# Turned inverse transform, half of x turned on TensorE, and denominators spread through DRAM, in a kernel of a long convolution beside linear attention

## The chip, the cores and the metric

The kernel runs on one core of one Trainium2 chip. The metric is the device time of one execution in microseconds (us); the median of several is quoted. A profiled execution gives the span, which is about 2 us shorter than the time. In some executions of this kernel the granted clock of TensorE is lower and the time longer by some per cent; those are called slow and are not compared with fast ones. A run counts as slow when it is over 1.5% above the fastest of the same kernel. SBUF and PSUM are the two on-chip memories in which the program places its buffers; its matmuls write to PSUM.

## The reference, cut to what matters

Two independent halves are computed and put side by side in the output. All inputs and outputs are bf16; S = 2048 and D = 576.

```python
# half A: a short filter on k, a product with v, a long convolution, a product with q
kv = k_shift * v                                   # k_shift: four taps along S
y  = irfft(rfft(kv, 2 * S) * rfft(ssm_k, 2 * S))[:S] + kv * ssm_D
a  = q * y
# half B: linear attention, 32 heads of 18
phi = lambda t: where(t > 0, t + 1, exp(t)) + 1e-6
num = phi(q) @ (phi(k)^T v)          # for each head
den = phi(q) @ sum_s phi(k) + 1e-6   # one denominator for each row and head
b   = (num / den) @ wo               # q, k, v = x @ wqkv
out = concatenate([a, b], axis=-1)
```

## The kernel before

The kernel issues its operations from a fixed list, `PLAN`. Each word names an engine and an operation (`P` TensorE, `A` ScalarE, `D` VectorE, `G` GpSimd, `S` the engine that issues transfers, SyncE); a second list, `PLACES`, gives each buffer its place. Each engine works through its own words in order, so an operation that waits holds up all later ones on its engine. This order was tuned.

Half A runs as two stages of matmuls with tables (forward, for the filter "h" and for the input "u"), a product, and two inverse stages. Between the two inverse stages the data are turned by a DMA transpose:

```python
def inv(g, su, bias):                       # first inverse stage, for one of nine pieces
    ...                                     # products of the two transforms: tx and xb
    V = SB("V", [128, 2, 8, 128])
    for jp in range(2):
        for wi, (w, src) in enumerate(((W31, tx), (W32, xb))):
            for h in range(2):
                for g2 in range(2):         # the small table is stationary: 64x64 tiles
                    nc.tensor.matmul(ps..., lhsT=w()[64 * h:64 * h + 64, :], rhs=v[:, g2, ...])
        ...                                 # evicted to V
    turn("Vtr", Vt[hf]..., V)               # DMA transpose

def inv2(hf, bias):                         # last inverse stage
    vt = Vt[hf].t[:].rearrange("p g (h r t) -> p r (g h) t", h=2, t=2)
    ...
    nc.tensor.matmul(o, lhsT=Esb.t[:, b, ri, :], rhs=vt[:, 2 * b + ri, :], ...)
```

In half B the projections need x turned, which comes by DMA transposes, and the reciprocals of the denominators (32 rows for each group of 512 columns) must be repeated 18 times over the partitions. Matmuls with a 0/1 table do that, into PSUM, from where the multiplication reads them:

```python
def b_bc(c, gp):
    ps = psb(2, "bps")
    for j in range(2):                      # "spreading" matmuls
        nc.tensor.matmul(ps.t[0:hn, j, :], lhsT=esel()[...], rhs=rden.t[...])
    # VectorE: pqT = (pqT + EPS) * spread reciprocal
    nc.vector.scalar_tensor_tensor(out=o, in0=o, scalar=EPS, in1=ps.t[0:hn], op0=ALU.add, op1=ALU.mult)
```

Each output projection ("out", ten matmuls) needs five of the ten multiplications, and each multiplication serves eight projections. GpSimd takes some of the products of half A; one takes it about 4 us, against 1.2 us on VectorE.

Of the kernel before, what the change touches and what calls it, by code (L numbers as in the profile page):

```python
# [9 lines left out]
BF = mybir.dt.bfloat16  # L10
# [108 lines left out]
def _tables():  # L119
# [35 lines left out]
    C = np.zeros((128, 224 + 128 + 630 + 32 + 160 + 126 + 8), np.float32)  # L155
    C[:, 0:32] = np.tile(W[:, 0], (4, 1))
    for r in range(2):
        for t in range(2):
            C[64 * r + t:64 * r + 64:2, 32 + 32 * t:64 + 32 * t] = W[:, 0]
            for i in range(2):  # L160
                C[64 * r + 32 * t:64 * r + 32 * t + 32, 96 + 64 * i + t:160 + 64 * i:2] = W[:, 1 + i]
    o = 224
# [35 lines left out]
def _act(n):  # L198
    return 0.17 + n * 0.000868


def _dve(n, rate=1):
    return 0.145 + n * 0.001045 / rate
# [6 lines left out]
def _dma(nb, row=4096):  # L210
    return nb / (16.0 * row / (8.0 + row * 0.0412) * 1000.0)
# [3 lines left out]
def kernel(  # L215
# [18 lines left out]
    G_d = nc.inline_tensor(Gt.reshape(128, -1), name="tab_g").ap()  # L234
# [32 lines left out]
    cst = SB("cst", [128, Ct.shape[1]], side=1, pre=True)  # L267
    neg1 = SB("neg1", [128, 1], FP32, side=1, pre=True)
    Gsb = SB("Gsb", [128, 16, 2, 128], side=1, pre=True)
# [11 lines left out]
    def cs(o, n):  # L281
        return cst.t[:, o:o + n]
# [3 lines left out]
    W31 = lambda: cs(96, 64)  # L286
    W32 = lambda: cs(160, 64)
    ident = lambda: cs(224, 128)
    esel = lambda: cs(352, 630).rearrange("p (c m) -> p c m", c=5)
    sel127 = lambda: cs(982, 32)  # L290
    hmask = lambda: cs(1014, 160).rearrange("p (c m) -> p c m", c=5)
    maskbd = lambda: cs(1174, 126)
    epsc = lambda: cs(1300, 1)
# [7 lines left out]
    xTg = []  # L301
    xTt = SB("xTt", [128, S])

    def xt_tail():
        load("xTt", xTt, lambda e: nc.sync.dma_start_transpose(out=xTt.t[:], in_=x[:, 448:576]), 524288,
             wr=[(xTt, "t")], issue=2.2, row=512, gap=0.5)
        P.op(("POOL", 0.9), lambda e: nc.gpsimd.memset(xTt.t[0:1, :], 1.0), rd=[(xTt, "t")], wr=[(xTt, "t")],
             name="xT1", bias=900)

    def xt_load(g):  # L310
        b = SB("xT%d" % g, [128, 4, 512])
        xTg.append(b)
        load("xT", b, lambda e: nc.sync.dma_start_transpose(
            out=b.t[:], in_=x[512 * g:512 * g + 512, 0:512]), 524288, wr=[(b, "m")], issue=2.2, row=512, gap=0.5)
# [41 lines left out]
    cload = load("cst", cst, lambda e: dma(cst.t[:], C_d), 128 * 2 * Ct.shape[1], bias=("cst", 0.0))  # L356
# [3 lines left out]
    for hh in range(2):  # L360
# [6 lines left out]
        P.op(("PE", 1.2), wmm, rd=[srow, ones], wr=[wps], name="wj", bias=("wall", 0.0), cnt=4)  # L367
# [3 lines left out]
    kv_load(0)  # L371
    xt_tail()
# [7 lines left out]
    load("Gsb", Gsb, lambda e: dma(Gsb.t[:].rearrange("p a b c -> p (a b c)"), G_d), 1048576)  # L380
# [37 lines left out]
    def h_piece(i):  # L418
# [3 lines left out]
        for half in range(2):  # L422
# [12 lines left out]
            P.op(("PE", 8 * 0.081), tr, rd=[hs, cst], wr=[ps], use=[hT[cc]], name="htr", cnt=8, bias=("t%d" % cc, 0.0))  # L435
# [9 lines left out]
    TX, seq = {}, {}  # L445

    def s1(cc, nm, bias):
        C = SB("C" + nm, [128, CC // 2, 32, 2])
        for ri in range(2):
            for bg in range(2):  # L450
                ps = psb(3, "s1ps")

                def mm(e, ri=ri, bg=bg, ps=ps):
                    for j in range(8):
                        b = 8 * bg + j
                        src = hT[cc].t[:, b, :] if nm == "h" else vs[bg].t[:, j, CC * cc:CC * cc + CC]
                        for bank, lo, hi in banks(CC * j, CC * j + CC):
                            nc.tensor.matmul(ps.t[:, bank, lo - 512 * bank:hi - 512 * bank], lhsT=Gsb.t[:, b, ri, :],  # L458
                                             rhs=src[:, lo - CC * j:hi - CC * j], start=True, stop=True)
# [7 lines left out]
                P.op(("PE", 0.72), mm, rd=rdk + [Gsb], wr=[ps], use=[C], name="s1" + nm, cnt=10, bias=bias)  # L467
# [3 lines left out]
    def turn(name, dst, src, rd, wr, bias):  # L471

        load(name, None, lambda e: nc.sync.dma_start_transpose(out=dst(), in_=src()), 524288, rd=rd, wr=wr, bias=bias,
             issue=2.2, row=512, gap=0.5)

    def s2(C, cc, pp, nm, bias):
        nw = PCH // 2
        if nm == "u":
# [7 lines left out]
        else:  # L486
            ct = SB("ctH", [128, 16, 128])
            turn("turn", lambda: ct.t[:],
                 lambda: C.t[:, nw * pp:nw * pp + nw].rearrange("p w r t -> p (w r t)"), [C], [ct], bias)
        g = cc * (CC // PCH) + pp  # L490
        sp = SB("sp" + nm, [128, 16, 128])
        for kp in range(2):
            ps = psb(2, "s2ps")

            def mm(e, kp=kp, ps=ps):
                if nm == "u":
                    for j in range(4):
                        for kk in range(2):
                            kh = 2 * kp + kk
                            w0 = 16 * (j // 2)  # L500
                            nc.tensor.matmul(ps.t[32 * j:32 * j + 32, kk, :].rearrange("p (w k) -> p w k", w=16),  # L501
                                             lhsT=W2()[32 * kh:32 * kh + 32, :],
                                             rhs=ct.t[32 * kh:32 * kh + 32, w0:w0 + 16, :, j % 2], start=True, stop=True)
                else:
                    for r in range(2):
                        for h in range(2):
                            b0 = 8 * h + 4 * kp
                            nc.tensor.matmul(ps.t[64 * h:64 * h + 64, r, :].rearrange("p (b k) -> p b k", b=4),  # L508
                                             lhsT=W2D()[64 * r:64 * r + 64, :],
                                             rhs=ct.t[64 * r:64 * r + 64, b0:b0 + 4, :], start=True, stop=True)  # L510

            def ev(e, kp=kp, ps=ps):
                if nm == "u":
                    copy(e, sp.t[:, :, 64 * kp:64 * kp + 64].rearrange("p w (h k) -> p h w k", h=2),
                         ps.t.rearrange("p h (w k) -> p h w k", w=16))
                else:
                    copy(e, sp.t[:, 8 * kp:8 * kp + 8, :].rearrange("p (b r) k -> p r b k", r=2),
                         ps.t.rearrange("p r (b k) -> p r b k", b=4))
            aft = [seq[x] for x in (nm, ("h", g)) if x in seq] if kp == 0 else []
            last = P.op(("PE", T8), mm, rd=[ct, cst], wr=[ps], use=[sp], name="s2" + nm, bias=bias, cnt=8 if nm == "u" else 4,  # L520
# [8 lines left out]
    Vt = [SB("Vt%d" % i, [128, VN[i] // 4, 128], side=1) for i in range(2)]  # L529

    def inv(g, su, bias):
# [4 lines left out]
        load("X", xb, lambda e: dma(xb.t[0:128:2], tx.t[1:128:2]), 262144, rd=[tx], wr=[(xb, 0)], bias=bias, row=4096)  # L536
        load("X", xb, lambda e: dma(xb.t[1:128:2], tx.t[0:128:2]), 262144, rd=[tx], wr=[(xb, 1)], bias=bias, row=4096)
# [6 lines left out]
        V = SB("V", [128, 2, 8, 128])  # L544
        for jp in range(2):
            ps = psb(2, "i1ps")

            def mm(e, jp=jp, ps=ps):
                for wi, (w, src) in enumerate(((W31, tx), (W32, xb))):
                    for h in range(2):  # L550
                        for g2 in range(2):
                            v = src.t[64 * h:64 * h + 64].rearrange("p (w g) k -> p g w k", g=2)
                            nc.tensor.matmul(  # L553
                                ps.t[64 * g2:64 * g2 + 64, h, :].rearrange("p (w k) -> p w k", w=4),
                                lhsT=w()[64 * h:64 * h + 64, :], rhs=v[:, g2, 4 * jp:4 * jp + 4, :],
                                start=(wi == 0), stop=(wi == 1))
            P.op(("PE", 2 * T8), mm, rd=[tx, xb, cst], wr=[ps], use=[V], name="i1", bias=bias, cnt=8)
            P.op(either(1024), lambda e, jp=jp, ps=ps: copy(
                e, V.t[:, :, 4 * jp:4 * jp + 4, :].rearrange("p h w k -> p h (w k)"), ps.t), rd=[ps], wr=[(V, jp)],
                name="i1ev", bias=bias)  # L560
        turn("Vtr", lambda: Vt[hf].t[:, c0 // 4:c0 // 4 + 16, :], lambda: V.t[:].rearrange("p h w k -> p (h w k)"),
             [V], [(Vt[hf], g)], bias)

    def inv2(hf, bias):
# [6 lines left out]
        for bg in range(16 // nb):  # L571
            ps = psb(2, "i2ps")

            def mm(e, bg=bg, ps=ps):
                vt = Vt[hf].t[:].rearrange("p g (h r t) -> p r (g h) t", h=2, t=2)
                for j in range(nb):
                    o = ps.t[:, j // (nb // 2), n * (j % (nb // 2)):n * (j % (nb // 2)) + n].rearrange(
                        "p (g t) -> p g t", t=2)
                    for ri in range(2):
                        b = nb * bg + j  # L580
                        nc.tensor.matmul(o, lhsT=Esb.t[:, b, ri, :], rhs=vt[:, 2 * b + ri, :],  # L581
# [6 lines left out]
            P.op(("PE", 1.6 * _pe(*[n] * (2 * nb))), mm, rd=[Vt[hf], Esb], wr=[ps], name="i2", cnt=2 * nb, bias=bias)  # L588
# [11 lines left out]
    def kproj(r):  # L600
# [10 lines left out]
        P.op(("PE", _pe(*[HALF] * 10)), mm, rd=[xTg[r // 4], xTt, wk], wr=[ps], use=[eb], name="k", bias=("k", 0.0), cnt=10)  # L611
# [8 lines left out]
    def qproj(c, gp):  # L620
# [9 lines left out]
        P.op(("PE", _pe(*[512] * 10)), mm, rd=[xTg[2 * gp], xTg[2 * gp + 1], xTt, wq],  # L630
# [14 lines left out]
    for c in range(5):  # L645
# [4 lines left out]
    load("x", x_sb, lambda e: dma(x_sb.t[:, :, 0:D], ap(x, 0, [[D, 128], [128 * D, 16], [1, D]])), 2359296, row=1152,  # L650
         wr=[(x_sb, "x")], after=[k_ids[AFTER["x"]]])
    P.op(("POOL", 0.3), lambda e: nc.gpsimd.memset(x_sb.t[:, :, D:D + 1], 1.0), wr=[(x_sb, "o")], name="x1",
         bias=400, after=[k_ids[AFTER["x"]]])
# [5 lines left out]
    def b_G(t):  # L659
# [7 lines left out]
        P.op(("PE", _pe(*[HALF] * 32)), mm, rd=[x_sb, pk], wr=[ps], use=[GT, gcol], name="G", cnt=32, bias=("G", 0.0))  # L667
# [36 lines left out]
    P.op(("PE", 25 * 0.081), kvmm, rd=[wv5, GT], wr=[kps], use=[kvb], name="kv", cnt=25, bias=("G", 0.0))  # L704

    def kvev(e):
# [3 lines left out]
    P.op(("DVE", _dve(504)), kvev, rd=[kps, cst], wr=[(kvb, 0)], name="kvev", bias=("G", 0.0))  # L710
    P.op(("DVE", _dve(72)), lambda e: nc.vector.tensor_tensor(
        out=kvb.t[0:72, 4, 0:72], in0=kps.t[0:72, 1, 0:72], in1=maskbd()[0:72, 0:72], op=ALU.mult),
        rd=[kps, cst], wr=[(kvb, 1)], name="kvev", bias=("G", 0.0))
# [6 lines left out]
    P.op(("PE", 0.4), zmm, rd=[(GT, 4), cst], wr=[zps], use=[zsel], name="z", cnt=5, bias=("z", 0.0))  # L720
# [7 lines left out]
    P.op(("DVE", 0.3), zev, rd=[zps, cst], wr=[zsel], name="zev", bias=("z", 0.0))  # L728
# [14 lines left out]
    P.op(("PE", 1.2), dmm, rd=[zsel, pqT, cst], wr=[dps], use=[den, dcol, rden], name="den", cnt=40, bias=("z", 0.0))  # L743
# [11 lines left out]
    def b_M(c):  # L755
# [7 lines left out]
        P.op(("PE", _pe(HALF, HALF)), mm, rd=[kvb, wo5], wr=[ps], use=[M], name="M", cnt=2, bias=("G", 0.0))  # L763
# [4 lines left out]

    def b_bc(c, gp):
        h0, hn = HCH[c]  # L770
        ps = psb(2, "bps")

        def mm(e):
# [136 lines left out]
```

## Time and profile before

| | before |
|---|---|
| time, median of 3 runs | 183.16 us (182.57 to 186.32; the last counts as slow) |
| span of the profiled run | 180.0 us |
| TensorE, VectorE, ScalarE, GpSimd busy | 161.2, 143.7, 109.8, 46.5 us |
| first matmul of k's projection | 17.23 us |
| first matmul of G = x^T phi(k) | 69.12 us |
| first output projection | 120.52 us |
| last matmul ends | 176.36 us |

In the views, PE is TensorE, PEld its weight loads, DVE VectorE, ACT ScalarE, POOL GpSimd and SP SyncE, and L607 is line 607 of that version's program. The busy time of an engine is read against the span; the windows show in which stage an engine is full; the chain of work that ended last shows what the end was waiting for. The four moments in the last rows cut the kernel into stages that can be compared between versions. "End minus first G" is used below as the length of the second part: here 180.03 - 69.12 = 110.91 us.

### The profile page before, as it was taken

The page shows a single profiled execution, that of the slowest core. Times are in us where ns is not written, and L with a number is a line of the kernel's source. Part 1 is how long each engine was busy: PE and PEld are TensorE (multiplying, and loading weights), DVE is VectorE, ACT ScalarE, POOL GpSimd, SP SyncE. Part 2 cuts the span into 40 slices and gives each one's busy share as a digit, 9 for nine tenths or more (in the row PEclk, how much of TensorE's full clock was granted, in tenths as well). Part 3 has the DMA queues.
Part 4 walks back from the last instruction along what each step waited for, and adds up shares of the span by engine and source line. Part 5 has one row for each costly group of instructions (what it writes and reads, how often), then busy time and mean ns, then how long its engine had stood idle before and what let it go on. Part 6 is the DMA issues. An engine that isn't in the chain of part 4 may idle for free.

```text
span 180.0 us, 3538 instructions
## 1 busy us (share of the span) xinstructions
PE 161.2 (90%) x1448; PEld 104.5 (58%) x1448; DVE 143.7 (80%) x136; ACT 109.8 (61%) x118; POOL 46.5 (26%) x29
## 2 busy tenths in 40 slices
PE   0795999999999979899999978788799999999991
PEld 0664677754766757676677745433348565554450
DVE  0307589898979899899969899996968999686863
ACT  2083364648856788755668889995958798620000
POOL 8004000150080340006304960653882000000000
PEclk9999799999999999999999999978969999999999
DMA  5999799999999944998096019979399983999844
GB/s 181 327 202 283 143 298 422 298 169 263 336 237 350 378 164 93 179 283 253 29 304 226 15 22 206 239 124 233 97 346 259 222 183 120 259 208 273 261 142 149
DMA packets 68886, 39.49 MB, mean 219 GB/s; under 512 B 50375, under 2 KB 66373, under 8 KB 68230
## 3 DMA queue, kind: packets, MB, share of 16 engines
q1 hardware_dynamic: 68870, 39.27, 84.9%
q8 instruction: 11, 0.18, 0.4%
q14 instruction: 5, 0.04, 0.1%
HBM read 17.77 MB, written 4.72 MB: 125 GB/s over the span
## 4 chain that ended last, share of the span: by engine, by line
PE 74%; DVE 9%; ACT 6%; DMA 6%; issue 2%; SPq 0%; DVEq 0%
PE ps_all L628 12%; PE ps_all L607 12%; PE ps_all L795 11%; PE ps_all L665 11%; PE ps_all L581 9%; PE ps_all L458 5%; PE ps_all L553 4%; PE ps_all L429 3%; DVE pqT L782 3%; DMA hs<-in_A_ssm_k_dram 3%; DMA wk<-in_B_wqkv_dram 3%; ACT Ch L253 2%; PE ps_all L508 2%; DVE Cu L255 2%; PE ps_all L501 2%
## 5 line engine op out<-in xcount | busy, mean ns | idle before, releaser
L407 POOL TENSOR_TENSOR v<-m,v 128x1536 bf16<-128x1536 bf16 x5 | 17.0, 3408 | 55.9 <-DVE m L404 26.2
L795 PE MATMUL ps_all<-M,pqT 126*128 126x288 bf16 (+1 forms) x160 | 24.3, 306 | 0.0
L253 ACT ACTIVATE sph<-ps_all 128x1024 bf16<-128x1024 f32 x18 | 18.0, 1022 | 8.4 <-PE ps_all L508 7.4
L607 PE MATMUL ps_all<-wk,xT 128*128 128x288 bf16 x128 | 21.4, 301 | 1.1 <-DMA wk<-in_B_wqkv_dram 1.1
L458 PEld LDWEIGHTS <-Gsb 128*128 128x128 bf16 x240 | 17.4, 102 | 7.4 <-issue 6.0
L396 DVE TENSOR_TENSOR m<-kh,Wj 128x3072 bf16<-128x3072 bf16 x12 | 20.8, 1748 | 0.9 <-DMA kh<-in_A_k_dram 0.9
L628 PE MATMUL ps_all<-xT,wq 128*126 128x512 bf16 (+1 forms) x80 | 20.7, 381 | 0.0
L665 PE MATMUL ps_all<-pk,x_sb 128*128 128x288 bf16 (+1 forms) x160 | 20.6, 287 | 0.0
L795 PEld LDWEIGHTS <-pqT 126*128 126x128 bf16 (+1 forms) x160 | 15.7, 103 | 8.3 <-issue 3.7
L253 ACT ACTIVATE spu<-ps_all 128x1024 bf16<-128x1024 f32 x16 | 15.8, 1026 | 4.9 <-PE ps_all L501 4.3
L665 PEld LDWEIGHTS <-x_sb 128*128 128x128 bf16 x160 | 15.3, 98 | 5.1 <-issue 1.3
L612 ACT ACTIVATE ek<-ps_all,neg 128x576 bf16<-128x576 f32 x16 | 11.8, 744 | 10.2 <-PE ps_all L607 5.3
L628 PEld LDWEIGHTS <-wq 128*126 128x126 bf16 (+1 forms) x100 | 12.7, 131 | 7.9 <-issue 0.9
L607 PEld LDWEIGHTS <-xT 128*128 128x128 bf16 x128 | 13.1, 103 | 5.5 <-issue 1.2
L581 PE MATMUL ps_all<-Vt,Esb 128*128 128x320 bf16 (+1 forms) x64 | 15.9, 421 | 0.0
L253 ACT ACTIVATE V<-ps_all 128x1024 bf16<-128x1024 f32 x13 | 12.9, 1022 | 4.1 <-PE ps_all L553 4.0
L632 ACT ACTIVATE eq<-ps_all,neg 126x1024 bf16<-126x1024 f32 (+1 forms) x10 | 11.1, 1112 | 6.4 <-PE ps_all L628 6.4
L586 DVE TENSOR_TENSOR q<-ps_all,q 128x640 bf16<-128x640 f32 (+1 forms) x12 | 11.2, 954 | 4.4 <-PE ps_all L581 4.4
L253 ACT ACTIVATE Ch<-ps_all 128x1536 bf16<-128x1536 f32 x9 | 13.0, 1501 | 1.8 <-PE ps_all L458 1.8
L615 DVE SCALAR_TENSOR_TENSOR pk<-ek,ps_all 128x576 bf16<-128x576 bf16 x16 | 11.8, 751 | 2.4 <-ACT ek L612 2.4
L635 DVE SCALAR_TENSOR_TENSOR pqT<-eq,ps_all 126x1024 bf16<-126x1024 bf16 (+1 forms) x10 | 12.2, 1215 | 1.7 <-ACT eq L632 1.5
L782 DVE SCALAR_TENSOR_TENSOR pqT<-pqT,ps_all 126x1024 bf16<-126x1024 bf16 (+1 forms) x10 | 11.9, 1212 | 1.6 <-PE ps_all L776 1.4
(77 smaller groups left out, 257.9 us busy)
## 6 DMA issues: line engine op xcount, KB each, us to landing
X<-sph SPq DMA_DIRECT2D x18, 256.0 KB, 3.9
hs<-in_A_ssm_k_dram SPq DMA_DIRECT2D x6, 384.0 KB, 4.1
v<-in_A_v_dram SPq DMA_DIRECT2D x2, 1152.0 KB, 9.6
x_sb<-in_B_x_dram SPq DMA_DIRECT2D x1, 2304.0 KB
out_dram<-ob SPq DMA_DIRECT2D x16, 144.0 KB, 3.1
kh<-in_A_k_dram SPq DMA_DIRECT2D x1, 1584.0 KB
q<-in_A_q_dram SPq DMA_DIRECT2D x1, 1280.0 KB
out_dram<-q SPq DMA_DIRECT2D x4, 320.0 KB, 2.6
```

What stands on the lines that cost most here:

```text
L253: nc.scalar.activation(out=o, in_=i, func=ACTF.Copy)
L396: nc.vector.tensor_tensor(out=m.t[:, i:i + 2], in0=i0, in1=i1, op=ALU.mult)
L407: lambda e: vec(e).tensor_tensor(out=vt.t[:, :, c0:c0 + CC], in0=m.t[:, 0], in1=vt.t[:, :, c0:c0 + CC], op=ALU.mult),
L458: nc.tensor.matmul(ps.t[:, bank, lo - 512 * bank:hi - 512 * bank], lhsT=Gsb.t[:, b, ri, :], rhs=src[:, lo - CC * j:hi - CC * j], start=Tru ...
L581: nc.tensor.matmul(o, lhsT=Esb.t[:, b, ri, :], rhs=vt[:, 2 * b + ri, :], start=(ri == 0), stop=(ri == 1))
L607: nc.tensor.matmul(ps.t[:, hh, 0:HALF], lhsT=xs(t, 128 * r, 128), rhs=wk.t[:, t, HALF * hh:HALF * hh + HALF], start=(t == 0), stop=(t == 4))
L612: P.op(("ACT", _act(576) + 0.085), lambda e: nc.scalar.activation(out=eb.t[:], in_=ps.t[:, :, 0:HALF], func=ACTF.Exp, bias=neg1.t[:]), rd= ...
L628: nc.tensor.matmul(ps.t[0:hn, j, :], lhsT=wq.t[:, t, h0:h0 + hn], rhs=xs(t, 1024 * gp + 512 * j, 512), start=(t == 0), stop=(t == 4))
L635: P.op(("DVE", _dve(1024)), lambda e: nc.vector.scalar_tensor_tensor(out=pqT.t[0:hn, c, 1024 * gp:1024 * gp + 1024].rearrange("p (h c) -> ...
L665: nc.tensor.matmul(ps.t[:, hh, 0:n], lhsT=x_sb.t[:, r, FT[t]:FT[t] + 128], rhs=pk.t[:, r, HALF * hh:HALF * hh + n], start=(r == 0), stop=( ...
L782: nc.vector.scalar_tensor_tensor(out=o, in0=o, scalar=EPS, in1=ps.t[0:hn], op0=ALU.add, op1=ALU.mult)
L795: nc.tensor.matmul(ps.t[:, hh, 0:HALF], lhsT=pqT.t[0:hn, c, 128 * r:128 * r + 128], rhs=M.t[0:hn, c, HALF * hh:HALF * hh + HALF], start=(c ...
```

## The change

The intent is to take work and hops off TensorE and the DMA queue. There are five parts.

1. In the first inverse stage the products become stationary and the table moves. The result comes out turned already, so the DMA transposes of V go, and the last inverse stage reads another layout.
2. The reciprocals are stored to DRAM and loaded back with a repeating address, in place of the spreading matmuls. The multiplication then reads them from SBUF.
3. "u" is turned on VectorE for six of nine pieces; the other three (`UT`) go by DMA transpose.
4. x is loaded early in its plain layout, its column of ones is written ahead of it, and the first half of it (`XP = 2` of four groups) is turned on TensorE.
5. The order and the places are made anew.

```diff
 def inv(g, su, bias):
-        V = SB("V", [128, 2, 8, 128])
         for jp in range(2):
-                for wi, (w, src) in enumerate(((W31, tx), (W32, xb))):
-                    for h in range(2):
-                        for g2 in range(2):
-                            nc.tensor.matmul(..., lhsT=w()[64 * h:64 * h + 64, :], rhs=v[:, g2, 4 * jp:4 * jp + 4, :], ...)
+                for j in range(8):
+                    for wi, src in enumerate((tx, xb)):
+                        nc.tensor.matmul(ps.t[:, j // 4, 128 * (j % 4):128 * (j % 4) + 128],
+                                         lhsT=src.t[:, 8 * jp + j, :], rhs=W3(wi), start=(wi == 0), stop=(wi == 1))
-        turn("Vtr", lambda: Vt[hf].t[:, c0 // 4:c0 // 4 + 16, :], ...)
 def inv2(hf, bias):
-                vt = Vt[hf].t[:].rearrange("p g (h r t) -> p r (g h) t", h=2, t=2)
+                vt = Vt[hf].t[:].rearrange("p r (g b t) -> p r b g t", g=2, t=2)
 ...
 def b_bc(c, gp):
-        ps = psb(2, "bps")
-            ... nc.tensor.matmul(ps.t[0:hn, j, :], lhsT=esel()[32 * g:32 * g + 32, c, 0:hn], rhs=rden.t[...])
+            bt = SB("bct", [128, 2, 512])
+            load("bc", bt, lambda e: dma(bt.t[0:hn]..., ap(
+                rdd, 14 * c * S + 1024 * gp, [[S, hn // 9], [0, 9], [1, 1024]])), ...)
-            nc.vector.scalar_tensor_tensor(out=o, in0=o, scalar=EPS, in1=ps.t[0:hn], op0=ALU.add, op1=ALU.mult)
+            nc.vector.scalar_tensor_tensor(out=o, in0=o, scalar=EPS, in1=bt.t[0:hn], op0=ALU.add, op1=ALU.mult)
 ...
 def xt_load(g):
+        if g >= XP: ... DMA transpose as before; return
+                        nc.tensor.transpose(out=..., in_=x_sb.t[:, 4 * g + 2 * hf + r, c0:c0 + 128], identity=ident())
 ...
+UT = (1, 4, 7)
+XP = 2
+BCD = 1
 PLAN = ...     # all words new
 PLACES = ...   # all places new
```

## The prediction

> **What bounds the kernel now.** I read the page first, then the table of windows, the chain of work that ended last, the groups by form, and last the timeline of the DMA-issuing queue. The page's first part says that TensorE is busy nine tenths of the time, and its second part says where it is not:
>
> ```profile
> PE 161.2 (90%) x1448; PEld 104.5 (58%) x1448; DVE 143.7 (80%) x136; ACT 109.8 (61%) x118; POOL 46.5 (26%) x29
> ...
> PE   0795999999999979899999978788799999999991
> PEclk9999799999999999999999999978969999999999
> ```
>
> The windows (window, length, then busy time of PE, PE weight loads, DVE, ACT, POOL, the granted clock, the DMA share and GB/s) put numbers on it:
>
> ```profile
> 0.00:17.20 17.20, 9.55 (x80) 7.54 (x81) 4.43 (x7) 7.05 (x6) 5.94 (x14) 1.00 0.92 245
> 17.20:69.30 52.10, 50.84 (x368) 35.16 (x368) 46.34 (x43) 33.38 (x37) 10.58 (x6) 0.97 0.96 269
> ...
> 98.50:131.00 32.50, 27.36 (x324) 15.22 (x325) 29.50 (x31) 28.98 (x29) 19.33 (x6) 0.93 0.65 135
> ...
> 155.80:176.40 20.60, 20.56 (x114) 10.36 (x110) 14.74 (x17) 2.05 (x2) 0.00 (x0) 1.00 0.94 220
> 176.40:180.00 3.60, 0.00 (x0) 0.00 (x0) 0.75 (x1) 0.00 (x0) 0.00 (x0) 1.00 0.40 122
> ```
>
> The reader is to see four stages. Until 17.2 us TensorE lacks 7.65 us. From there to 98 us it is full. From 98.5 to 131 us it lacks 5.1 us while VectorE (29.5 of 32.5) and ScalarE (29.0) are both nearly full, and its clock is lowered. The tail from 155.8 us is TensorE alone; after it comes one eviction and one store, 3.6 us. The chain says what ends the first stage and what makes the tail:
>
> ```profile
> 12.48 4.71 DMA wk<-in_B_wqkv_dram
> ...
> 17.23 11.63 PE ps_all L607 x80
> ...
> 160.58 14.54 PE ps_all L581 x60
> ```
>
> The weights of k hold the first projection, and the issuing queue shows why they are late: they are issued at 12.48 us, after two DMA transposes of x have held the queue for 8 us.
>
> ```profile
> 4.36 5.64 SPq L313 DMA_TRANSPOSE xT<-in_B_x_dram  x1
> 10.12 2.31 SPq L305 DMA_TRANSPOSE xTt<-in_B_x_dram  x1
> 12.48 0.59 SPq L245 DMA_DIRECT2D wk<-in_B_wqkv_dram  x1
> ```
>
> The groups that the change touches on TensorE and VectorE:
>
> ```profile
> L553 PE MATMUL ps_all<-sph,cst 64*64 64x512 bf16 x72 | 7.4, 403 | 0.5 <-DVE pqT L782 0.3
> L482 DVE STREAM_TRANSPOSE ct<-Cu 128x1024 f32<-128x1024 f32 x9 | 10.7, 1222 | 0.1
> L581 PE MATMUL ps_all<-Vt,Esb 128*128 128x320 bf16 (+1 forms) x64 | 15.9, 421 | 0.0
> L776 PE MATMUL ps_all<-rden,cst 32*126 32x512 bf16 (+1 forms) x20 | 4.3, 421 | 1.3 <-ACT Ch L253 0.5 <-DVE pqT L782 0.4 <-ACT V L253 0.3
> L702 PE MATMUL ps_all<-GT,wv 128*126 128x126 bf16 (+1 forms) x25 | 1.5, 217 | 0.0
> ```
>
> The number ahead of the comma is busy time with overlaps counted once; the mean beside it includes the pipeline's depth and is no pace.
>
> **What the Trainium skill says.** "TensorE: Matmul & The Clock Gate", section "Wait — 56ns, not 53.3ns?": warm matmuls start N/2.4 ns plus about 2.5 ns apart. The trace agrees: in the chain 20 projections of 288 columns take 2.45 us, 122.5 ns each, which is 288/2.4 + 2.5. "SBUF — State Buffer", section "Door 1: The DMA port swizzle": SBUF is read in 16-byte lines, and an access that crosses into a new line pays. The trace agrees for the last inverse stage (L581): its moving operand is read as pairs of bf16 at 128-byte steps, and 60 matmuls of 288 columns on average take 14.54 us, 242 ns each, twice 122.5. "VectorE: DVE Perf Modes", section "The three transpose paths": VectorE turns 32x32 blocks only, TensorE and the DMA crossbar turn 128x128 ones, TensorE into PSUM. So turning x on TensorE costs evictions too. "DMA: Bandwidth & Descriptors", section "Anatomy of one DMA — SWDGE (gpsimd) path": a transfer, there of the other kind of queue, has a fixed cost near 2 us, most of it the write receipt. Here the 144 KB stores land 3.1 us after issue (median), so the trip of the denominators through DRAM is two such times, about 6 us before the first multiplication can use it.
>
> **The change part by part.**
>
> Start. The loads are put in a new order: direct loads first, DMA transposes later, the tables cut in pieces, and x itself early. Half of x is turned on TensorE instead of by DMA. Ahead of the end of the k weights the new queue has 0.79 MB of filter rows, 0.12 of constants, 0.26 of table, 0.88 of x, 0.66 of weights: 2.71 MB. The page's row of rates gives 181 and 327 GB/s in the first two 4.5 us slices, 2.28 MB by 9 us; 0.43 MB more at 300 and about 1 us to land make 11 us. So the first k matmul moves from 17.2 to about 11 us, 6.2 us. But before, four groups of the first transform stage (10 matmuls, 0.67 us each) were done by then, and now one is: 2.0 us are owed later. The new turns of x are 40 transposes of 128 columns; 30 of them lie ahead of the first k, inside the 11 us, and 10 cost 10 x 57 ns = 0.6 us. Net **-3.6 us**.
>
> First inverse stage (L553). Before, the tables were stationary and 144 matmuls of 512 columns ran as four 64x64 tiles side by side; the window sum of this line is 10.35 us. Now the products are stationary: 18 x 16 = 288 matmuls of 128 columns on the whole array, each with a fresh stationary operand. The nearest row of the same kind is L702, where 25 matmuls of about 126 columns, each with fresh weights, take 1.5 us, 57 to 60 ns each. 288 x 57 ns = 16.4 us: **+6.1 us** on TensorE. What it buys: the result comes out turned, so the nine DMA transposes of V (5.0 us to landing) vanish, and with them the hop between this stage and the last.
>
> Last inverse stage (L581). 64 matmuls stay. One row of the moving operand now lies in n consecutive elements, read as pairs alternating between its two halves, so each 16-byte line serves four near reads. Unhindered it would take 64 x 122.5 ns = 7.8 us, as now 15.9. I choose 1.3 times the unhindered, 10.2 us: **-5.7 us**. This is my least certain term: 0 to -8.
>
> Denominators. The 20 spreading matmuls go (4.35 us busy): **-4.3 us**. In their place two stores of 128 KB and ten loads of about 250 KB. VectorE's multiplication (1.21 us) reads SBUF instead of PSUM; I expect the same duration. By the order of instructions, some 20 us of other TensorE work stand between the denominators' matmuls and the first output projection, more than the 3.4 us reciprocal, 6 us of DRAM and five multiplications of 1.2 us, so the trip is hidden.
>
> u by DMA for three of nine: 3 x 1.22 us less on VectorE, against about 2 us of evictions of turned x. No direct effect on TensorE.
>
> Stalls from 98.5 to 131 us. 5.1 us idle, and two output groups at half clock (ten matmuls in 2.52 and 2.48 us instead of 1.25) give 2.5 us more. They come of evictions and PSUM buffers passed between full engines; fewer hops, no spreading matmuls that wait for PSUM, and an earlier start of VectorE should give back about half: **-4 us**. New waits, on the DMA queue above all: **+1 us**.
>
> Sum: -3.6 + 6.1 - 5.7 - 4.3 - 4 + 1 = -10.5 us on 183.2: about **173 us**.
>
> **Rivals.** One: the last inverse stage still pays a line for each pair, so the -5.7 is 0 and TensorE has more work than before; then about 178 us. For it: pairs still alternate between two places. Against: the lines are shared by neighbours now, before they were not. Two: VectorE is the bound (143.7 us busy, 9.3 tenths from 30 to 120 us) and hardly loses work; then only its earlier start counts, some 5 us, and the time is about 178. For it: the stage from 98.5 us. Against: in the tail VectorE has slack. Three: the queue of DMA issues, which is in order, stalls on the denominators' store or on x's later transposes, behind 7.8 MB of loads (about 30 us), so that the q projections of the second half of x wait; then 176 to 182. For it: the DMA share is 0.96 in the second window. Against: nine transposes fewer. Four: everything fits and the middle loses nearly no stalls: 168.
>
> **Range and chances.** Terms that are sure in sign (start, spreading matmuls, first inverse stage) sum to -1.8; the gain rests on the last stage and the stalls, each uncertain by about 4 us. That gives 168 to 179. Slower by over 2% needs both to fail and a new wait: 0.03. Within 2%, above 179.5 us: 0.10. Faster: 0.87.
>
> **What would show it.** In the changed profile: first k projection near 11 us; the last inverse stage near 10 us busy; the first near 16; no spreading matmuls; PE idle time in the middle cut to half; TensorE's total busy time about 160 us (161.2 with the terms above and 2.3 us of turned x). The prediction is wrong if the last stage still takes 15 us, if the first k projection is later than 14 us, or if the output projections wait for the multiplied q.

## The result, and the profile after

The changed kernel takes 176.5 us (median of 4 runs, 175.78 to 177.1). The four runs of the kernel before took 182.57, 183.16, 185.84 and 186.32 us; the last two count as slow, so their median of 184.5 us is not used. The ratio of the fast runs is 0.965, with a 95% interval of 0.9582 to 0.9719: faster by 3.5%, or 6.4 us of 182.87 (the mean of the two fast runs). The span of the profiled runs, both fast, went from 180.0 to 174.6 us, a gain of 5.4 us. The prediction had 10.5 us.

The page of the changed kernel, its busy times and then the busy tenths and granted clock of TensorE in 40 slices:

```profile
PE 157.6 (90%) x1588; PEld 117.2 (67%) x1588; DVE 146.9 (84%) x140; ACT 112.5 (64%) x122; POOL 42.1 (24%) x28
...
PE   0979999999999988999998898891999999999992
...
PEclk9999999999999999999999999997599999999999
```

TensorE's busy time fell by 3.6 us and VectorE's rose by 3.2 us; one slow instruction, shown below, adds 3.9 us to the latter. There is one hole in TensorE's row, the slice marked 1 (118 to 122 us), and in that slice and the next the clock falls (7 and 5 tenths). The windows of the changed kernel (window, length, busy time of PE, weight loads, DVE, ACT, POOL, clock, DMA share, GB/s), chosen as those of before:

```profile
0.00:17.20 17.20, 11.71 (x107) 9.83 (x108) 4.26 (x9) 8.11 (x10) 6.03 (x15) 1.00 0.94 282
17.20:69.30 52.10, 50.94 (x393) 36.36 (x391) 51.19 (x48) 37.81 (x41) 12.33 (x7) 1.00 0.99 242
98.50:131.00 32.50, 26.43 (x311) 17.52 (x309) 29.79 (x24) 26.36 (x28) 10.09 (x2) 0.89 0.79 195
```

In the second window VectorE is now full: 51.19 of 52.10 us, where it had 46.34. In the third, TensorE lacks 6.1 us, more than the 5.1 us of before, and the mean clock is 0.89 where it was 0.93. The chain of work that ended last in the changed kernel (start, length, what):

```profile
3.60 6.77 DMA x_sb<-in_B_x_dram
10.41 2.31 PE ps_all L343 x20
12.73 1.28 PE ps_all L510 x10
14.01 0.61 PE ps_all L343 x10
14.62 1.23 PE ps_all L654 x10
...
20.90 1.77 DVE m L447
...
115.37 6.14 DVE pqT L838 x2
121.56 1.86 PE ps_all L851 x7
...
162.93 5.73 PE ps_all L628 x40
```

Three things are to be seen. The start is now held by the load of x and by its turns (L343), not by the weights of k; the first matmul of k (L654) comes at 14.46 us. From 20.9 to 56 us the chain runs through VectorE. And two multiplications (L838) that should take 2.4 us took 6.1, and the last seven matmuls of the first output projection (L851) follow them. The groups that answer to those shown of before (busy time, mean ns of one, idle before):

```profile
L603 PE MATMUL ps_all<-cst,sph 128*128 128x128 bf16 x144 | 17.1, 219 | 0.0
...
L838 DVE SCALAR_TENSOR_TENSOR pqT<-pqT,bct 126x1024 bf16<-126x1024 bf16 (+1 forms) x10 | 15.5, 1601 | 0.0
...
L343 PE MATMUL ps_all<-cst,x_sb 128*128 128x128 bf16 x40 | 4.0, 269 | 0.9 <-DMA x_sb<-in_B_x_dram 0.9
...
L536 DVE STREAM_TRANSPOSE ct<-Cu 128x1024 f32<-128x1024 f32 x6 | 7.4, 1233 | 0.0
...
L628 PE MATMUL ps_all<-Vt,Esb 128*128 128x320 bf16 (+1 forms) x64 | 10.3, 317 | 0.0
```

The spreading matmuls are gone. The last inverse stage (L628) took 10.3 us where it took 15.9. The multiplications took 15.5 us where they took 11.9 in the kernel before; all of the surplus is in one instruction. The changed kernel, the source line of the multiplication (ns: least, median, most; starts of the first and last):

```profile
L838 DVE SCALAR_TENSOR_TENSOR pqT<-pqT,bct x10: 1210/1215/5079, 107.8 to 137.9; 126x1024 bf16<-126x1024 bf16 x8, 72x1024 bf16<-72x1024 bf16 x2
```

And its timelines of VectorE and GpSimd there (start, length, engine, what, and the idle time before it):

```profile
115.29 6.21 DVE L838 SCALAR_TENSOR_TENSOR pqT<-pqT,bct 126x1024 bf16<-126x1024 bf16 x2
115.45 4.97 POOL L592 TENSOR_TENSOR X<-spu,X 128x2048 bf16<-128x2048 bf16 x1 [9.10 <-DVE spu L256]
```

The first of the two multiplications took 1.21 us. GpSimd's product, which began during it, took 4.97 us and ended at 115.45 + 4.97 = 120.42 us. The second multiplication took 5.08 us and ended at 115.29 + 6.21 = 121.50, about one ordinary multiplication after GpSimd had finished. The table of waits gives the price on TensorE, 3.7 us for the output projections. In the kernel before, the same pair of operations lay side by side without harm, with the reciprocals in PSUM; the same views of before:

```profile
117.65 3.69 DVE L782 SCALAR_TENSOR_TENSOR pqT<-pqT,ps_all 126x1024 bf16<-126x1024 bf16 x3
119.13 4.06 POOL L542 TENSOR_TENSOR sph<-spu,sph 128x2048 bf16<-128x2048 bf16 x1 [2.86 <-ACT spu L253]
```

Three multiplications in 3.69 us are 1.23 us each, and GpSimd's product kept its 4.06 us.

### The profile page after: what moved, and what is told of

It is laid out like the page before. It is cut to its first block, busy times and chain, and to the rows that moved or that the text cites. A ratio compares the mean times of both kernels' runs of the same rounds, so it can differ in the third digit from the quotient of the medians.

```text
span 174.6 us, 3816 instructions
## 1 busy us (share of the span) xinstructions
PE 157.6 (90%) x1588; PEld 117.2 (67%) x1588; DVE 146.9 (84%) x140; ACT 112.5 (64%) x122; POOL 42.1 (24%) x28
## 4 chain that ended last, share of the span: by engine, by line
PE 54%; DVE 31%; ACT 5%; DMA 4%; issue 3%; SPq 1%; DVEq 0%; ACTq 0%
PE ps_all L851 12%; PE ps_all L708 9%; PE ps_all L603 8%; PE ps_all L510 6%; PE ps_all L628 6%; DVE pqT L682 5%; DVE m L447 5%; DVE pk L662 5%; DVE pqT L838 4%; DMA x_sb<-in_B_x_dram 4%; DVE m L452 3%; PE ps_all L654 3%; PE ps_all L675 3%; PE ps_all L561 2%; PE ps_all L343 2%
## 5 line engine op out<-in xcount | busy, mean ns | idle before, releaser
L851 PE MATMUL ps_all<-M,pqT 126*128 126x288 bf16 (+1 forms) x160 | 23.1, 300 | 4.0 <-DVE pqT L838 3.7
L851 PEld LDWEIGHTS <-pqT 126*128 126x128 bf16 (+1 forms) x160 | 15.7, 102 | 11.0 <-DVE pqT L838 4.0
L595 POOL TENSOR_TENSOR sph<-spu,sph 128x2048 bf16<-128x2048 bf16 x3 | 15.4, 5118 | 32.3 <-ACT spu L254 29.6
L458 POOL TENSOR_TENSOR v<-m,v 128x1536 bf16<-128x1536 bf16 x4 | 12.4, 3099 | 42.4 <-DVE m L455 42.4
L447 DVE TENSOR_TENSOR m<-kh,Wj 128x3072 bf16<-128x3072 bf16 x12 | 20.8, 1752 | 0.1
L654 PE MATMUL ps_all<-wk,xT 128*128 128x288 bf16 x128 | 20.1, 286 | 0.1
L254 ACT ACTIVATE sph<-ps_all 128x1024 bf16<-128x1024 f32 x16 | 16.2, 1033 | 2.6 <-PE ps_all L561 2.4
L254 ACT ACTIVATE ob<-ps_all 128x576 bf16<-128x576 f32 x14 | 9.2, 664 | 12.6 <-PE ps_all L851 11.8
L254 ACT ACTIVATE Ch<-ps_all 128x1536 bf16<-128x1536 f32 x10 | 15.0, 1513 | 3.2 <-PE ps_all L510 3.1
L603 PE MATMUL ps_all<-cst,sph 128*128 128x128 bf16 x144 | 17.1, 219 | 0.0
L603 PE MATMUL ps_all<-cst,X 128*128 128x128 bf16 x144 | 17.0, 219 | 0.0
L254 ACT ACTIVATE Vt<-ps_all 128x1024 bf16<-128x1024 f32 x12 | 11.9, 1030 | 7.5 <-PE ps_all L603 7.5
L254 ACT ACTIVATE Cu<-ps_all 128x1536 bf16<-128x1536 f32 x10 | 14.9, 1538 | 2.3 <-PE ps_all L510 2.3
L838 DVE SCALAR_TENSOR_TENSOR pqT<-pqT,bct 126x1024 bf16<-126x1024 bf16 (+1 forms) x10 | 15.5, 1601 | 0.0
L654 PEld LDWEIGHTS <-xT 128*128 128x128 bf16 x128 | 12.3, 98 | 3.8 <-issue 0.4
```

What stands on the lines that cost most here:

```text
L254: nc.scalar.activation(out=o, in_=i, func=ACTF.Copy)
L447: nc.vector.tensor_tensor(out=m.t[:, i:i + 2], in0=i0, in1=i1, op=ALU.mult)
L458: lambda e: vec(e).tensor_tensor(out=vt.t[:, :, c0:c0 + CC], in0=m.t[:, 0], in1=vt.t[:, :, c0:c0 + CC], op=ALU.mult),
L595: lambda e: vec(e).tensor_tensor(out=tx.t[:], in0=su.t[:], in1=tx.t[:], op=ALU.mult),
L603: nc.tensor.matmul(ps.t[:, j // 4, 128 * (j % 4):128 * (j % 4) + 128], lhsT=src.t[:, 8 * jp + j, :], rhs=W3(wi), start=(wi == 0), stop=(wi ...
L654: nc.tensor.matmul(ps.t[:, hh, 0:HALF], lhsT=xs(t, 128 * r, 128), rhs=wk.t[:, t, HALF * hh:HALF * hh + HALF], start=(t == 0), stop=(t == 4))
```

## The experiments

The question is where the other half of the expected gain went. My theory is a collision: the multiplication now has both operands in SBUF and must wait while GpSimd reads there. The rival is that VectorE's total work, or the order of it, sets the time, and that the slow multiplication is only where this shows. In the expectations of the first four runs the collision is theory A and the rival is theory B. The runs e1 to e4 were made on one chip beside 7 runs of the kernel before (median 182.24 us), e5 to e8 on a second, e9 to e11 on a third.

### e1_changed: the changed kernel again

No edit. It gives the level for the runs beside it.

> The changed kernel itself, once more, so that the other runs of this call have it beside them on the same chip. Both theories: 0.96 to 0.97 of the kernel before, and again one of the ten multiplications of q by the denominators at about 5 us while a product of GpSimd runs.

Measured: 176.33 us, ratio 0.9651 (0.958 to 0.9722). The first result is confirmed on another chip. End minus first G is 106.53 us (107.27 in the first profile).

### e2_product_on_vector: one product moved from GpSimd to VectorE

```diff
-... A457 G426 D347 P256 ...
+... A457 D426 D347 P256 ...
```

Operation 426 is the product at 115.45 us; only its engine is changed.

> One of the four products that GpSimd makes is given to VectorE at the same place of the order; nothing else is changed. Theory A (the 5.08 us multiplication is held by GpSimd, because both of its operands now lie in SBUF): all ten multiplications take 1.21 to 1.25 us, TensorE's 3.7 us wait for the multiplied q is gone or under 0.5 us, the clock between 120 and 130 us stays near 1.0, VectorE has one product of 1.2 us more, and the time is 2 to 4 us under the changed kernel (172.5 to 174.5). Theory B (the multiplication waits for its own load or for something else): the 5 us stays, and the time is the same or 1 us longer.

Measured: 171.08 us (170.21 to 171.33), ratio 0.9357 (0.9289 to 0.9425), 5.25 us less than e1 by the medians, and under the 172.5 to 174.5 us that theory A expected. The source line of the multiplication, and the window from 98.5 us, in e2:

```profile
L838 DVE SCALAR_TENSOR_TENSOR pqT<-pqT,bct x10: 1210/1214/1216, 107.6 to 132.8; 126x1024 bf16<-126x1024 bf16 x8, 72x1024 bf16<-72x1024 bf16 x2
...
98.50:131.00 32.50, 29.32 (x372) 20.97 (x370) 31.55 (x30) 31.38 (x34) 5.12 (x1) 1.00 0.84 208
```

Every multiplication is back at 1.21 us, although VectorE has 1.2 us more to do. TensorE issues 372 matmuls in the window instead of 311, at a granted clock of 1.00 instead of 0.89. The gain is more than the wait of 3.7 us that was taken away; the fall of the clock is gone as well. Two groups shortly after the wait, 8 and 10 matmuls at 122.84 and 123.84 us in e1, took 1.07 and 2.56 us there; in e2 the same groups took 0.63 and 1.41. With these 1.6 us the account comes to 5.3. The other runs agree: each profile with GpSimd's product beside the multiplication from SBUF (the first one, e1, e4, e7, e8) has a mean granted clock of 0.98 to 0.991, each without that product (e2, e5, e6, e9, e10, e11) one of 0.996 or more. The rival, by which more work on VectorE should not help, is refuted as the main cause. This version beats both kernels.

### e3_denominators_by_matmul: the spreading matmuls put back

```diff
-BCD = 1
+BCD = 0
```

The store and the ten loads leave `PLAN`; ten pairs of spreading matmuls are placed by hand, each ahead of its multiplication, in PSUM banks that are free there.

> The denominators are spread by 20 matmuls into PSUM again, as in the kernel before; the rest is the changed kernel, GpSimd's products included. Theory A: the multiplications read PSUM and take 1.21 us each even beside GpSimd; TensorE has 4 us more of matmuls and loses 3.7 us of waiting, so the time is within 1.5 us of the changed kernel. Theory B (the trip through DRAM saves what the matmuls cost): 3 to 5 us slower than the changed kernel.

Measured: 188.71 us (186.62 to 188.94), ratio 1.0305 (1.0217 to 1.0394). Both theories' times are missed by far. The multiplications themselves, though, behave as the collision theory says. The timelines of VectorE and GpSimd in e3:

```profile
119.16 4.06 POOL L592 TENSOR_TENSOR X<-spu,X 128x2048 bf16<-128x2048 bf16 x1 [12.05 <-DVE spu L256]
119.60 1.22 DVE L838 SCALAR_TENSOR_TENSOR pqT<-pqT,ps_all 126x1024 bf16<-126x1024 bf16 x1 [0.52 <-PE ps_all L832]
121.57 1.22 DVE L838 SCALAR_TENSOR_TENSOR pqT<-pqT,ps_all 126x1024 bf16<-126x1024 bf16 x1 [0.74 <-PE ps_all L832]
```

With the reciprocals in PSUM, two multiplications lie wholly inside GpSimd's product and all three operations keep their ordinary length. So it is the place of the operand, not the neighbourhood, that costs. The 12.4 us on top of e1 come with waits in both directions: VectorE waits 7.1 us in all for the spreading matmuls, and these wait for PSUM to be evicted (the longest, 1.0 us, for VectorE). How much of that belongs to spreading by matmul, and how much to an order that I made by hand and did not tune, stays open; this run does not price the DRAM trip.

### e4_u_all_on_vector: all nine pieces of u turned on VectorE

```diff
-UT = (1, 4, 7)
+UT = ()
-... S406 ... S453 ... S500 ...
+... D406 ... D453 ... D500 ...
```

> All nine pieces of u are turned on VectorE, none by DMA. If VectorE sets the pace between 20 and 150 us, where it is 9.3 to 10 tenths busy: three transposes of 1.23 us make it 2 to 4 us slower than the changed kernel. If TensorE alone sets the pace: within 0.7 us of it.

Measured: 178.44 us (177.27 to 179.32), ratio 0.9747 (0.9661 to 0.9834), which the record calls unclear against the kernel before. Against e1 the runs do not overlap. Three transposes of 1.23 us, 3.7 us in all, cost 2.1 us against e1. End minus first G is 109.16 us against 106.53 in e1, so the cost lies in the second part. VectorE does help to set the pace there, and the rival is right that far. The collision stays, with a slowest multiplication of 4.15 us. In this order, part 3 of the change was worth having, where the prediction had given it no direct effect.

### e5_no_product_on_gpsimd: the other three products moved too

```diff
-... G401 ... G414 ... G426 ... G521 ...
+... D401 ... D414 ... D426 ... D521 ...
```

> All four products that GpSimd makes go to VectorE, at their places in the order. If the one that met the multiplications was the whole loss, the other three now only load VectorE, which is 31.5 of 32.5 us busy between 98.5 and 131 us: 1 to 3 us slower than the run with one product moved (172 to 174). If the sharing costs all along (GpSimd's products last 5.1 and 6.4 us beside VectorE instead of 4.06), it is 1 us or more faster than that run.

Measured: 172.47 us (170.65 to 172.65). The runs of the kernel before were disturbed (181.01 to 258.24 us; five of seven were slow, three of them at a clock of 0.94 and one at 0.57), so no ratio was formed, and I compare the stages: end minus first G is 102.71 us, against 102.06 in e2. The other three products are neither the loss nor much of a help; they do not lie beside a multiplication. The comparison is across chips.

### e6_x_first: the load of x ahead of the second half of the filter

```diff
-G30 S280 S8 S286 G31 S60 G5 G14 S6 S57 G9 G1 S23 G3 S25 P10 ...
+G5 G9 S280 S8 S6 S23 S25 S286 S60 S57 G30 G31 G14 G1 G3 P10 ...
```

It is e2 with x loaded earlier, and with x's turns moved between the two groups of filter turns on TensorE.

> On top of the one product on VectorE: x's first two loads are issued ahead of the second filter rows, the diagonal row and the table; the ones are written first on GpSimd; TensorE turns x between the two pairs of filter turns. If x's landing (10.4 us) and the turning after it hold the first k projection (14.5 us), it comes at about 12.5 us and the end 1 to 2 us earlier (169 to 170). If the k weights hold it, the first projection and the time stay within 0.7 us.

Measured: 174.32 us (173.75 to 174.44), no ratio. x was turned from 8.33 us on instead of 10.32 in e2, but the first k came at 16.65 us, where e2 had 14.01, because the filter's second half now came late and its work stands ahead of k in TensorE's order. Both theories' numbers were missed. End minus first G is 102.08 us, as in e2, so all of the loss is in the start. VectorE's first long product with the taps came 3.65 us later than in e2 (20.74 against 17.09), and the first G 3.43 us later (70.59 against 67.16).

### e7_rows_in_one_run and e8_rows_in_steps: the layout that the last stage reads

These two take the 16-byte-line argument apart. The changed kernel reads pairs of bf16 that alternate between two places. e7 reads the same elements in one run; e8 reads pairs at steps of 128 bytes, as the kernel before did. In both the columns come in another order than the right one, so they are only for timing. The comparison with the reference let both pass: the values of half A have a root mean square of 3.8e-7, those of half B of 2.0e-3, so an error in half A is not seen in a comparison of the whole. For the other runs too, the comparison says nothing of half A; that e10's order of columns, below, is right rests on its access patterns.

```diff
 # e7
-    rhs=vt[:, 2 * b + ri]
+    rhs=Vt[hf].t[:, 2 * b + ri]
 # e8
-    vt = Vt[hf].t[:].rearrange("p r (g b t) -> p r b g t", g=2, t=2)
+    vt = Vt[hf].t[:].rearrange("p r n -> p (r n)").rearrange("p (b g r t) -> p r b g t", g=2, r=32, t=2)
```

> Wrong result on purpose (columns in another order). The changed kernel, with the moving operand of the last inverse stage read as one run of n elements instead of pairs from two halves. If 16-byte lines set the pace: 136 and 109 ns per matmul of 320 and 256 columns, the stage 8.4 us busy instead of 10.3. If the fresh stationary operand sets it: 170 and 136 ns as now, 10.3 us.

> Wrong result on purpose. The changed kernel, with the same operand read as pairs 128 bytes apart, as the kernel before did. If 16-byte lines set the pace: 270 and 218 ns per matmul and 16 us busy, the time 4 to 6 us over the changed kernel. If the new layout has nothing to do with the gain: 10.3 us busy.

Measured, in one run each, whose state is therefore unknown: 176.17 us for e7 and 182.54 us for e8. The paces below are read inside the traces and do not depend on the total. The groups of the last stage, first of e7 and then of e8 (busy time, mean ns):

```profile
L628 PE MATMUL ps_all<-Vt,Esb 128*128 128x320 bf16 x32 | 5.0, 299 | 0.0
L628 PE MATMUL ps_all<-Vt,Esb 128*128 128x256 bf16 x32 | 3.7, 272 | 0.0
```

```profile
L628 PE MATMUL ps_all<-Vt,Esb 128*128 128x320 bf16 x32 | 9.1, 447 | 0.0
L628 PE MATMUL ps_all<-Vt,Esb 128*128 128x256 bf16 x32 | 7.1, 395 | 0.0
```

The starts of the 320-column matmuls lie 136 ns apart in e7, 170 in the changed kernel and 271 in e8: one run, alternating pairs, pairs at large steps. The stage is busy 8.65, 10.29 and 16.11 us. Undoing the layout alone therefore gives back 5.8 us on TensorE, and end minus first G grows to 112.28 us, from 106.5 to 107.3 in two other runs of the changed kernel. So the gain of this stage seems to lie on the path nearly whole, as far as one run can tell.

### e9, e10 and e11: how far the better version goes

e9 is e2 again. e10 adds to e9 a right version of the single run: the moving operand is read in one run, and the order of the columns is set on the way out, in pairs of fp32 written to PSUM at steps of 16 bytes. e11 adds to e10 an earlier first k: x is loaded ahead of the first transform's table, and k's first projection stands directly behind the turn that it needs.

```diff
 # e10, on top of e9
-    vt = Vt[hf].t[:].rearrange("p r (g b t) -> p r b g t", g=2, t=2)
+    vt = Vt[hf].t[:].rearrange("p r (g b t) -> p r g b t", g=2, t=2)
-    o = ps.t[:, j // (nb // 2), n * (j % (nb // 2)):n * (j % (nb // 2)) + n]
+    o = ps.t[...same...].rearrange("p (b g t) -> p g b t", g=2, t=2)
 # e11, on top of e10: the head of PLAN
-G30 S280 S8 S286 G31 S60 G5 G14 S6 S57 G9 G1 S23 G3 S25 P10 ...
+G5 G9 S280 S8 S286 G30 G31 S6 S25 G14 S23 S60 S57 G1 G3 P10 ...
-... P48 P46 ... P34 S52 A49 P36 D291 D47 A35 P294 D37 P38 P32 A295 S53 P110 ...
+... P48 P46 ... P36 S52 A49 P38 D291 D47 D37 A39 P110 P294 P34 P32 A295 A35 ...
```

> The run with one product moved to VectorE once more, as the neighbour of the next two on the same chip: 0.93 to 0.945 of the kernel before.

> On top of the one product on VectorE: the last inverse stage reads its moving operand as one run of n elements, and puts the columns in order by writing PSUM in pairs of fp32 at 16-byte steps; the result is right. If only the read counts: 136 and 109 ns per matmul, the stage 8.6 us busy, and the end up to 1.6 us earlier than the run beside it, less where VectorE's products with q (11 us) set the tail. If PSUM writes in pairs cost as much as reads in pairs: 10 us busy or more, and no gain.

> On top of the run before this: x's first loads go ahead of the diagonal row and the table, the ones are written first, and on TensorE the first k projection comes right after the turn of its own tokens, ahead of the first transform group. If the in-order stream of TensorE (turns, their evictions, the transform group) held the first k projection: it comes at 11.5 to 12.5 us instead of 14, and the end 0.5 to 1.5 us earlier. If the k weights hold it: 13.5 to 14 us, nothing gained.

Measured, beside 8 runs of the kernel before, of which the four slow ones are left out of the ratios (the record calls all three verdicts unclear, although the intervals lie under 0.98):

| run | time, us | ratio | end minus first G, us |
|---|---|---|---|
| e9 | 171.58 | 0.9477 (0.9389 to 0.9564) | 102.08 |
| e10 | 171.71 | 0.9489 (0.9417 to 0.9562) | 101.50 |
| e11 | 170.67 | 0.9438 (0.9375 to 0.9501) | 101.60 |

e9 is within 0.5 us of e2; its ratio lies just outside the expected 0.93 to 0.945, and the two intervals overlap. e10 saves 1.64 us of TensorE work (8.65 us busy against 10.29) and shortens the second part by 0.6 us only. VectorE's last six products with q stand back to back there (159.67 to 165.97 us), but the chain does not pass through them, so why so little comes of it is not shown. In e10's profile the first G is also 1.25 us later than in e9's, because VectorE waited 1.64 us for the load of v. e11 has the most to say. Its timelines of TensorE at the first k, of ScalarE at the exponential of that k (L659) and at the eviction ahead of it, and of VectorE at the first long product with the taps (L447):

```profile
11.36 1.12 PE L654 MATMUL ps_all<-wk,xT 128*128 128x288 bf16 x4
...
14.19 1.47 ACT L254 ACTIVATE Ch<-ps_all 128x1536 bf16<-128x1536 f32 x1 [2.50 <-PE ps_all L510]
...
16.09 0.74 ACT L659 ACTIVATE ek<-ps_all,neg 128x576 bf16<-128x576 f32 x1
...
17.60 1.75 DVE L447 TENSOR_TENSOR m<-kh,Wj 128x3072 bf16<-128x3072 bf16 x1
```

k came at the 11 us that the prediction had named, 3.1 us earlier than in the changed kernel. But VectorE's first long product starts at 17.60 us, and in the changed kernel it starts at 17.48 us:

```profile
17.48 1.75 DVE L447 TENSOR_TENSOR m<-kh,Wj 128x3072 bf16<-128x3072 bf16 x1
...
20.00:56.00 36.00, 36.00 (x259) 25.43 (x256) 35.31 (x35) 23.58 (x28) 8.71 (x5) 1.00 1.06 245
```

k did not reach VectorE any earlier, though. The first ten matmuls of k end at 13.49 us instead of 15.85, while their exponential starts at 16.09 us (15.97 in the changed kernel). In ScalarE's order the eviction of a transform group still stands ahead of that exponential, and on TensorE the edit had put this group behind k. The first product of VectorE with the exponential waits for it, and the long product stands behind that one. So e11 does not test what an earlier k gives when the exponential comes earlier too; that stays open.

What the runs do show is that the first G follows VectorE. From 20 to 56 us VectorE of the changed kernel is busy 35.31 of 36 us (31.81 in the kernel before), and in e11 35.24. The first G comes 49.8 to 50.1 us after the first long product in the changed kernel, e1, e2, e3, e6, e9 and e11, although k starts between 11.36 and 16.65 us in them. In e4, e5, e7, e8 and e10 it comes 51.0 to 51.8 us after it, and there VectorE waited 1.1 to 1.6 us for the load of v. The gain of 1 us of e11 over e9 and e10 lies inside the intervals.

## Why the prediction was right and where it was off

The time came out inside the range, and the change is faster by over 2%. The gain is 5.4 us by the spans and 6.4 by the fast runs, half to six tenths of what was forecast. The terms:

| term | predicted, us | measured, us |
|---|---|---|
| start | -3.6 | -1.8 (first G 69.12 to 67.34) |
| first inverse stage | +6.1 | +7.2 (10.35 to 17.57 busy) |
| last inverse stage | -5.7 | -5.65 (15.94 to 10.29 busy) |
| spreading matmuls | -4.3 | -4.35 (4.35 to 0 busy) |
| stalls, and new waits | -4 + 1 | -0.8 (what is left of -5.4) |

The last row is the measured gain of the span less the sum of the other rows. Busy time taken off TensorE need not all lie on the path, so this remainder is an account and no measurement.

**The last inverse stage was right** in mechanism and in size, and e7 and e8 show the mechanism: only the layout of the moving operand differs, and the pace runs from 136 to 271 ns. The term that I had called the least certain was the best one. My factor of 1.3 over the unhindered pace measured 1.25 (170 over 136 ns).

**The spreading matmuls were right** as TensorE time. **The first inverse stage** was mis-sized by 1.1 us. The pace was as predicted: a group of 16 matmuls starts 56 ns apart. The difference is in the ends of the 18 groups: 288 matmuls of 57 ns are 16.4 us, and the busy time of 17.57 counts each group's pipeline running out.

**The start failed as a step.** The prediction took the first k projection for the thing that starts everything, and expected it at 11 us; it came at 14.46. x landed at 10.4 us, and its turns and one group of the transform stood ahead of k. It also sized the turning of x at 57 ns each, 2.3 us in all, and the 40 took 4.0 us busy: the first 20 took 2.31 us, later tens 0.61 and 0.70. The deeper fault is the step from "k earlier" to "the stage is shorter by as much, less the work that is owed". VectorE sets the end of that stage, and its first long product moved from 18.99 to 17.48 us only, 1.5 us, close to the 1.8 us by which the first G moved. That product had started 1.76 us after the first k in the kernel before; now it started 3.02 us after it, behind the exponential of that k. e6 shows both late together, and e11 an early k with the exponential and the long product where they were. Rival two, that VectorE is the bound and about 178 us come out, was right for this stage, and I gave it too little weight. e4 says the like of the second part: three transposes on VectorE, to which I had given no direct effect, were worth 2.1 us.

**The stalls failed, and this is the larger part.** The prediction said: "VectorE's multiplication (1.21 us) reads SBUF instead of PSUM; I expect the same duration." Nine of ten kept it; one took 5.08 us, the output projections waited 3.7 us for it, and the clock fell at that time. The trip through DRAM was hidden, as predicted (0.0 us of idle ahead of the ten multiplications); the reader of what it brought was not. I had counted what the operand's move saves on TensorE and in PSUM, and not asked who else reads in its new place. The Trainium skill would have told it: "SBUF — State Buffer", section "Who interferes with whom", says that a VectorE instruction with two SBUF inputs contends with a GpSimd instruction that reads SBUF, and that the port pair they share is an exclusive lock. The trace agrees on both sides. GpSimd's product, begun under the first multiplication, took 4.97 us instead of 4.06; the second multiplication then took 5.08 us and ended 1.08 us after it. e3 shows no such delay with the operand in PSUM, and e2 none without GpSimd's product. With that one product moved, the profiled span is 169.2 us, 10.8 us less than before on another chip. That this is so near the predicted 10.5 is in part luck: by the same account the start gave 2.0 us instead of 3.6, the first inverse stage cost 1.1 more, and the remainder, -6.1 us where the prediction had -3, makes up for both.

Of the signs that the prediction itself named as proof against it, two came: k later than 14 us, and output projections that wait for the multiplied q. The third did not: the last stage does not take 15 us. Its total for TensorE, about 160 us, measured 157.6; that too is partly luck, since 161.2 with the measured terms would make 162.4. The idle time in the middle was to be halved and grew, from 5.1 to 6.1 us. Rival one fell with the last stage. Rival three, a stall of the DMA queue, shows nowhere in the changed kernel's chain after the first load of x, though the time of 176.5 us lies in its range; the nearest to it are VectorE's waits for v in five other runs. Rival four, 168 us, was not reached by any version run here; the best, e11 and e2, stand at 170.67 and 171.08 us on different chips.

## What to carry to other kernels

When an operand moves from PSUM to SBUF, ask what else reads SBUF at that moment: a multiplication with two SBUF operands beside one GpSimd product cost 3.7 us of waiting and a lowered clock here, and moving that one product off GpSimd (1.2 us on VectorE) won 3.0% over the changed kernel (0.9357 over 0.9651). Before pricing an earlier start by the first instruction that starts earlier, look for the engine that is full in that stage, and ask when its work starts and what stands ahead of it in its own order. A new layout for a matmul's moving operand is worth a small timing run of its own: the same 64 matmuls took 8.65, 10.29 and 16.11 us here.

## What the Trainium skill lacked or had wrong

- "SBUF — State Buffer", section "Door 1: The DMA port swizzle": its note names two hits or more in a 16-byte line as the condition for full bandwidth. Two were not enough here: pairs of bf16 at 128-byte steps, two elements in each line, took 271 ns for a matmul of 320 columns, 2.0 times the 136 ns of one run. Pairs that alternate between two runs took 170 ns, 1.25 times. The note gives no sizes for its penalty.
- The same note says that any non-contiguous PSUM pattern slows matmuls significantly. In e10 the output was written in pairs of fp32 at 16-byte steps, and the pace was 136 and 109 ns for 320 and 256 columns, as with e7's contiguous output: no slowing.
- "SBUF — State Buffer", section "Who interferes with whom": it gives no measured size for a two-input VectorE operation beside a GpSimd product. Here the multiplication took 5.08 us instead of 1.21, and GpSimd's product 4.97 instead of 4.06.
